# Scaled states on GpSimd, the output of the first units in two PSUM banks, and a new order of steps up to unit 6

## The chip, the core and the metric

The kernel runs on one core of a Trainium2 chip. TensorE (PE) multiplies, VectorE (DVE), ScalarE (ACT) and GpSimd (POOL) work elementwise, and the queue of SyncE (SP) issues nearly all DMA transfers. The metric is the device time of one execution in microseconds (us); less is better.

## The reference

A state-space attention (Mamba-2 style) of 4 batch rows, 8 heads, 768 tokens, head size 32 and state size 16, followed by a feed-forward layer with tanh-gelu on 3072 tokens:

```python
log_a = np.log(np.clip(a, 1e-06, 1.0))
for c in range(nc):                          # chunks of the sequence
    cum = np.cumsum(la, axis=-1)
    L = np.exp(cum[:, :, :, None] - cum[:, :, None, :]) * causal
    M = np.einsum('bhin,bhjn->bhij', Cc, Bc) * L
    y_intra = np.einsum('bhij,bhjd->bhid', M, xc)
    y_inter = np.einsum('bhin,bhnd->bhid', Cc, state) * np.exp(cum)[..., None]
    y[:, :, sl] = y_intra + y_inter
    state = decay_full * state + sum_over_j(B_j x_j * decay_from_j)
x = y.transpose(0, 2, 1, 3).reshape(3072, 256)
h = x @ w_in                                 # 256 -> 2048
g = 0.5 * h * (1.0 + np.tanh(c * (h + 0.044715 * h * h * h)))
out = g @ w_out                              # 2048 -> 256
```

Inputs and output are 32-bit floats; the products run in bf16 with 32-bit accumulation.

## The kernel before

The sequence is cut into 24 **chunks** of 128 tokens, 6 in each batch row, and 12 **units** of two chunks. Unit `u` holds chunks `2u` and `2u+1`; units 0 to 2 are batch 0, 3 to 5 batch 1, and so on. The decays are folded into B and C beforehand: a scan along the tokens gives the products of `a`, which scale B (with their value) and C (with their reciprocal).

The program is one list of steps, the string `ORDERED`. Each step issues its instructions on its engine when its turn comes, so the list sets the order of every engine and of SP's queue. A step's name is its function and its arguments; `:A`, `:D`, `:P`, `:S` after it name the engine (ACT, DVE, POOL, SP), and `@a`, `@b`, `@o`, `@y` the PSUM bank that it takes. Without a name, steps that ask for a passing bank get `bank_b` and `bank_a` in turn (`take`). Waits follow from what each instruction reads and overwrites.

The steps of unit `u`, with the lines of the profile:

- `G.u` (L637, L644, PE): products of B and C for 8 heads into the banks `ga` and `gb`. It needs `ce`, the masked C, and `bh`, B.
- `M.u.0`, `M.u.1` (L654, DVE): the causal mask on `ga` and on `gb`, to `m`.
- `castx.u` (L350, L352): x to bf16; `x` of units 0 and 1 is made on PE instead (`XX`, `XD`, `xn`).
- `D.u` (L679, PE): what the two chunks add to the state, from `bn` (B with tokens on the partitions) and x.
- `S.u.k` (L750, L752, DVE): the state after chunk `2u+k`. `SP.c` (L759, DVE): the state after chunk `c`, scaled by the decay and spread through the block mask `bmask` to 256 columns, so that one matmul on all 128 rows takes the part of one head. It needs `pendq` (chunks 0 to 2) or `pend`.
- `Y.u` (L701, L710, PE) for units 0 to 3: `m` times x, plus the state times `ce`, both into `bank_y`; `yev` (L348, ACT) copies it to `xm`. From unit 4 on `Yi` (L721) and `YI` (L734) do this for two units at once, in two banks.
- `s1.u.i` (L790 for units 0 to 3, L795 after): four matmuls of 256 columns (two of 512 later) with `w_in`; `gelu.u.i` (L801, L804, ACT) moves the result to `gT`; `s2.u.k.q` (L816) is a quarter of the product with `w_out` for chunk `k`: four matmuls of 256 columns; `oev.c` and `store.c` bring chunk `c` out.

Weights are loaded (`load_wi`, `load_wo`) and cast to bf16 (`wi`, `wo`). `s1.u.6` and `s1.u.7` need the last quarter of `w_in`.

The B and C of chunks 4 and 5 have steps of their own: the scan `R` (L365), its transpositions `tp2` and `tp6` (L375), `recip1`, the products `mul1.0` and `mul1.1` (L470), `T1.0`, `T1.1` (L478) and `N1` (L498) on PE, and the copies `ce1`, `bh1`, `bn1`; `pe`, `pp` and `pend` make the chunk-end decays of chunks 3 on. For batch 1 the steps are `mul`, `T`, `E`, `F`, `N`. For batches 2 and 3 they go through memory: `mul.b.1` and `mul.b.0` (L510) scale C and B, `load_wr.b.i` (L524) writes each to a scratch tensor, `load_tr.b.1` and `load_tr.b.0` (L531) read them back transposed as `ch` and `bh`, `load_bn.b` (L536) reads `bn`, and `F.b` (L549, DVE) makes `ce` from `ch`. `G.6` needs `ce` and `bh` of batch 2, `D.6` its `bn`; `D.9` is the first to need `bn` of batch 3.

`hold` (L630, GpSimd) copies one column of a scaled state, so that what follows on GpSimd waits for it.

Of the kernel before, what the change touches and what calls it, by code (L numbers as in the profile page):

```python
# [22 lines left out]
xn.2 s1.0.0 G.1 S.1.0 s1.0.1 xn.3 gelu.0.0 gelu.0.1 s1.0.2 gelu.0.2 M.1.1 wi.2.0 M.1.0 s1.0.3 gelu.0.3
s1.0.4 s1.0.5 recip1 S.1.1 gelu.0.4 gelu.0.5 SP.1 load_wi.3 wi.3.1 wi.3.0 load_bc1.1 s1.0.6 load_bc1.0
mul1.0:P SP.2 pe mul1.1:P T1.0 bh1:D tp6 Y.1 gelu.0.6 pp load_wo.0 pend:D yev.1.0.2 T1.1 N1 wo.0.0 s1.0.7
load_x.2 ce1.1:D castx.2.None ce1.0:D recip.1 s1.1.0 bn1 SP.3 gelu.0.7 wo.0.1 G.2 D.2 gelu.1.0 S.2.0
s1.1.1 gelu.1.1 s2.0.0.0 s1.1.2 gelu.1.2 s1.1.3 load_bc.1.1 SP.4 load_bc.1.0 M.2.1 M.2.0 gelu.1.3
load_wo.1 s2.0.1.0 mul.1.0 s1.1.4 hold.4 mul.1.1:P recip.2 load_x.3 gelu.1.4 wo.1.0 s1.1.5 wo.1.1 Y.2
gelu.1.5 castx.3.None s1.1.6 yev.2.0.2 T.1.0 s1.1.7 gelu.1.6 load_wo.2 E.1.0 T.1.1 s1.2.0 N.1 gelu.1.7
gelu.2.0 E.1.1 bn.1:D s1.2.1 F.1 s2.0.0.1 wo.2.0 wo.2.1:D s1.2.2 gelu.2.1 s2.0.1.1 D.3 G.3 S.3.0 gelu.2.2  # L30
s1.2.3 gelu.2.3 S.3.1 M.3.0 M.3.1 load_wo.3 load_x.4 wo.3.0:A s2.0.0.2 s2.0.1.2 wo.3.1 SP.6 s1.2.4 s1.2.5
castx.4.None s2.0.0.3 s2.0.1.3 gelu.2.4 gelu.2.5 oev.0:D s1.2.6 load_bc.2.1 load_bc.2.0 load_x.5 load_x.6
oev.1 SP.7 G.4 gelu.2.6 D.4 Y.3 yev.3.0.2:A s1.2.7 s2.1.0.0@o mul.2.1:P S.4.0 s2.1.1.0@y load_wr.2.1
s2.1.0.1 load_x.7 mul.2.0:P load_wr.2.0 load_tr.2.1 recip.3 load_bn.2 S.4.1 SP.9 M.4.1 load_tr.2.0
s2.1.0.2 gelu.2.7 s1.3.0 gelu.3.0 s1.3.1 s2.1.1.1 load_bc.3.1 gelu.3.1 s2.1.0.3 M.4.0 s1.3.2
castx.6.None:D load_bc.3.0 gelu.3.2 s1.3.3 gelu.3.3 s2.1.1.2 s2.1.1.3 s1.3.4 mul.3.1:P castx.5.None:D G.5
M.5.1 store.0 oev.2:A oev.3:A D.5 S.5.0 gelu.3.4 SP.10 s2.2.1.0@o load_x.8 store.1 s2.2.0.0@y s2.2.0.1
s2.2.0.2 SP.8 s1.3.5 gelu.3.5 s2.2.0.3 s1.3.6 castx.7.None:D M.5.0 gelu.3.6 s2.2.1.1 s2.2.1.2 store.3
s1.3.7 F.2 oev.4:A gelu.3.7 load_wr.3.1 load_x.9 Yi.4@ya Yi.5 YI.4 YI.5 G.6 D.6@b D.7 yew.4.1 s2.2.1.3
oev.5:D yew.4.0 s1.4.0@a S.6.0 S.6.1 S.7.0 s2.3.0.0@y gelu.4.0 S.7.1 M.6.0 SP.13 M.6.1 store.2 s1.4.1@o  # L40
mul.3.0:D load_wr.3.0 castx.8.None:D gelu.4.1 load_tr.3.1 s2.3.0.1 s1.4.2@a SP.12 s1.4.3@b s1.4.4@o
gelu.4.3 gelu.4.4 load_bn.3 gelu.4.2 load_tr.3.0 s2.3.0.2 s2.3.0.3 oev.6:A load_x.10 s1.4.5@b s1.4.6@o
# [24 lines left out]
oev.22:D store.22 oev.23:A store.23
# [15 lines left out]
def kernel(  # L83
# [113 lines left out]
    held = const.tile([128, 1], BF16, name="held")  # L197
# [430 lines left out]

    def f_hold(c):
        nc.gpsimd.tensor_copy(out=held, in_=state[("sp", c)][:, 0:1])  # L630
# [39 lines left out]
    def f_D(u):  # L670
# [3 lines left out]
        for k in range(2):  # L674
# [3 lines left out]
            for g in range(4):  # L678
# [404 lines left out]
```

## Time and profile before

| | us |
|---|---|
| three timed runs | 116.06, 116.80, 118.12 |
| median of them | 116.8 |
| span of the profiled execution, first to last instruction | 116.7 |
| PE busy in it | 107.8 |
| ACT busy | 69.8 |
| DVE busy | 66.2 |
| GpSimd busy | 24.8 |

No time of the profiled execution is given apart from its span; the span is 0.1 below the median of the timed runs. In a row of the profile `L816` is a line of the kernel, `out<-in` are its tiles, `x4` is the number of instructions merged into the row, and the brackets at a row's end hold the idle time before it and what ended that. PE's matmuls overlap, so what a step costs on PE is the distance from its start to the next one's, not the duration in its row. SPq is the queue of SP: its rows are the issuing of transfers, not the transfers.

### The profile page before, as it was taken

How to read it: one execution, taken by the hardware profiler on the slowest of the kernel's cores; microseconds unless marked ns; L12 is line 12 of the kernel's file. 1: busy time of each engine (PE TensorE's matmuls, PEld its weight loads, DVE VectorE, ACT ScalarE, POOL GpSimd, SP SyncE). 2: the span in 40 equal slices, each digit the busy share in tenths (PEclk: the TensorE clock that was granted, in tenths of full speed). 3: DMA queues.
4: the chain of work that ended last, by engine and by line, in shares of the span. 5: the costliest groups of instructions: out<-in, count | busy, mean ns of one | idle time of the engine just before them, and what ended most of it. 6: DMA issues, size and time to landing. Idle time of an engine off the chain costs nothing.

```text
span 116.7 us, 3120 instructions
## 1 busy us (share of the span) xinstructions
PE 107.8 (92%) x1276; PEld 77.6 (66%) x1284; DVE 66.2 (57%) x136; ACT 69.8 (60%) x135; POOL 24.8 (21%) x53
## 2 busy tenths in 40 slices
PE   6989758799999999999999999999999999999990
PEld 2345547588788969665766775777657676777870
DVE  3799995699899279399806901928614521011010
ACT  4179675587575655469774688834775565763500
POOL 7644737455526400050010200000000000000000
PEclk9999999999999999999999999999999999999999
DMA  0999949996997787895978802220000013301032
GB/s 26 254 313 314 305 81 239 286 230 178 296 249 117 144 168 152 201 248 170 217 145 142 169 3 93 96 90 6 0 0 0 0 51 123 101 0 45 6 135 90
DMA packets 43102, 15.99 MB, mean 137 GB/s; under 512 B 36688, under 2 KB 41552, under 8 KB 43088
## 3 DMA queue, kind: packets, MB, share of 16 engines
q1 hardware_dynamic: 42992, 15.76, 54.9%
q8 instruction: 10, 0.16, 0.7%
q10 hardware_dynamic: 96, 0.03, 0.1%
q14 instruction: 4, 0.03, 0.1%
HBM read 11.07 MB, written 3.93 MB: 129 GB/s over the span
## 4 chain that ended last, share of the span: by engine, by line
PE 52%; SPq 27%; DMA 14%; issue 2%; ACT 2%; DVE 0%; DVEq 0%
PE bank_y L816 13%; PE bank_o L816 12%; SPq L175 10%; PE bank_b L795 8%; SPq L194 7%; PE bank_a L795 6%; DMA wf<-in_moe_w_in_dram 5%; SPq L168 5%; DMA x_t<-in_x_dram 4%; PE bank_o L795 3%; DMA scr<-bc 2%; DMA bn<-scr 2%; PE bank_y L795 2%; PE bank_b L816 2%; PE bank_a L816 1%
## 5 line engine op out<-in xcount | busy, mean ns | idle before, releaser
L816 PEld LDWEIGHTS <-gT 128*128 128x128 bf16 x384 | 37.1, 98 | 10.4 <-issue 0.6
L816 PE MATMUL bank_o<-w_out_sb,gT 128*128 128x256 bf16 x192 | 26.1, 273 | 0.0
L816 PE MATMUL bank_y<-w_out_sb,gT 128*128 128x256 bf16 x160 | 21.2, 273 | 0.1
L795 PEld LDWEIGHTS <-w_in_sb 128*128 128x128 bf16 x128 | 14.2, 114 | 7.5 <-issue 0.4
L804 ACT ACTIVATE gT<-bank_b 128x512 bf16<-128x512 f32 x25 | 14.9, 597 | 6.5 <-PE bank_b L795 6.1
L654 DVE TENSOR_TENSOR m<-ga,tri 128x1024 bf16<-128x1024 f32 x12 | 14.6, 1218 | 5.2 <-PE gb L637 5.2
L804 ACT ACTIVATE gT<-bank_a 128x512 bf16<-128x512 f32 x21 | 12.6, 599 | 6.8 <-PE bank_a L795 2.5
L790 PEld LDWEIGHTS <-w_in_sb 128*128 128x128 bf16 x128 | 13.5, 114 | 4.1 <-POOL w_in_sb L350 1.6
L801 ACT ACTIVATE gT<-bank_b 128x512 bf16<-128x512 f32 x17 | 10.1, 597 | 8.7 <-PE bank_b L790 8.6
L795 PE MATMUL bank_b<-xm,w_in_sb 128*128 128x512 bf16 x48 | 14.5, 380 | 0.2
L654 DVE TENSOR_TENSOR m<-gb,tri 128x1024 bf16<-128x1024 f32 x11 | 13.4, 1216 | 0.0
L790 PE MATMUL bank_b<-xm,w_in_sb 128*128 128x256 bf16 x68 | 10.3, 274 | 1.7 <-POOL w_in_sb L350 1.3
L795 PE MATMUL bank_a<-xm,w_in_sb 128*128 128x512 bf16 x36 | 11.2, 380 | 0.1
L352 DVE COPY o_sb<-bank_y 128x256 f32<-128x256 f32 x5 | 2.1, 425 | 15.7 <-PE bank_y L816 13.7
L801 ACT ACTIVATE gT<-bank_a 128x512 bf16<-128x512 f32 x15 | 8.9, 595 | 3.4 <-PE bank_a L790 3.3
L790 PE MATMUL bank_a<-xm,w_in_sb 128*128 128x256 bf16 x60 | 9.0, 273 | 0.9 <-ACT gT L801 0.4
L759 DVE SCALAR_TENSOR_TENSOR sp_new<-s_new,pend,bmask 128x256 bf16<-128x256 f32 x17 | 8.2, 497 | 0.3 <-DVE s_new L752 0.2
L352 DVE CAST xm<-bank_a 128x512 bf16<-128x512 f32 x4 | 2.8, 692 | 9.7 <-PE bank_a L734 9.7
L773 PE MATMUL bank_y<-wz 128*128 128x512 bf16 (+2 forms) x20 | 7.1, 499 | 1.1 <-DVE warm L225 1.1
L510 POOL TENSOR_TENSOR bc<-bc_t,pt 128x768 bf16<-128x768 f32 x3 | 4.7, 1563 | 14.6 <-PE bank_o L795 11.6
L804 ACT ACTIVATE gT<-bank_o 128x512 bf16<-128x512 f32 x10 | 6.0, 597 | 2.4 <-PE bank_o L795 2.3
L348 ACT ACTIVATE xm<-bank_y 128x512 bf16<-128x512 f32 x8 | 4.8, 596 | 3.8 <-PE bank_a L734 3.5
(149 smaller groups left out, 130.9 us busy)
## 6 DMA issues: line engine op xcount, KB each, us to landing
out_dram<-o_sb SPq DMA_DIRECT2D x24, 128.0 KB, 1.8
x_t<-in_x_dram SPq DMA_DIRECT2D x20, 128.0 KB, 4.3
wf<-in_moe_w_in_dram SPq DMA_DIRECT2D x4, 512.0 KB, 6.4
wf<-in_moe_w_out_dram SPq DMA_DIRECT2D x4, 512.0 KB, 6.5
bc_t<-in_C_dram SPq DMA_DIRECT2D x3, 384.0 KB, 6.9
bc_t<-in_B_dram SPq DMA_DIRECT2D x3, 384.0 KB, 6.3
scr<-bc SPq DMA_DIRECT2D x4, 192.0 KB, 3.0
x_t<-in_x_dram SPq DMA_DIRECT2D x1, 512.0 KB, 5.0
```

The lines of the kernel that those rows point to most:

```text
L168: nc.sync.dma_start(out=d["bc"][:, i], in_=(B, C)[i][b].rearrange("h (p r) n -> p h (r n)", r=R6))
L175: (nc.scalar if eng == "ACT" else nc.sync).dma_start(out=XF[u][:, k], in_=x[b, :, (c + k) * Q:(c + k + 1) * Q, :].rearrange("h p d -> p h d"))
L194: nc.sync.dma_start(out=WF[("o", q)], in_=wo[q])
L352: nc.vector.tensor_copy(out=o, in_=i)
L654: nc.vector.tensor_tensor(out=m_of(u)[:, 2 * i:2 * i + 2].rearrange("p g k e t -> p (g k e) t"), in0=gx[i].rearrange("p g (k t) -> p (g k) ...
L759: nc.vector.scalar_tensor_tensor(out=sp_new.rearrange("p (g d) -> p g d", g=4), in0=(XN[0][:, H * D:H * D + 64] if gc == 0 else state[("s" ...
L773: nc.tensor.matmul(out=t[:, 0:m * 128], lhsT=wz, rhs=w3.to_broadcast([128, m, 128]), start=True, stop=True, skip_group_check=True)
L790: nc.tensor.matmul(out=hp[:, j * T:(j + 1) * T], lhsT=w_in_k[:, w, q, k], rhs=xm[:, w, u * T:(u + 1) * T], start=(w == 0), stop=(w == 1))
L795: nc.tensor.matmul(out=hp, lhsT=w_in_k[:, w, q, k], rhs=xm[:, w, u * T:u * T + PT], start=(w == 0), stop=(w == 1))
L801: nc.scalar.activation(gts[u][:, 2 * i:2 * i + 2], hp.rearrange("p (j t) -> p j t", j=2), AF.Gelu_apprx_tanh)
L804: nc.scalar.activation(gts[("p", u)][:, i], hp, AF.Gelu_apprx_tanh)
L816: nc.tensor.matmul(out=ops[gc], lhsT=gts[u][:, fi, k * Q:(k + 1) * Q], rhs=w_out_sb[:, fi, :], start=(fi == 0 and (u > 0 or k == 0)), stop ...
```

## The change

Four things change; everything from `Yi.4` on stands in the order of before.

- `SP` of chunks 1 to 4 no longer spreads the state through the mask. It scales the 64 columns alone, on GpSimd. The matmuls that use it take 32 rows of it each, at the row group of their head.
- `Y` of units 0 to 2 goes into two banks, one for heads 0 to 3 and one for heads 4 to 7, and `yev` is two copies, one on ACT and one on DVE.
- The scan `R` stands behind the masks of unit 1 (`M.1.1`, `M.1.0`) on DVE.
- The list of steps up to `Yi.4` is in a new order. The `s1` steps of units 0 to 3 take four banks by name, and those of unit 1 begin before those of unit 0 have ended. `hold` is gone.

```diff
-xn.0:D load_wi.2 SP.0 ~13 Y.0 wi.0.1:A wi.0.0:A S.0.0 clip R S.0.1 yev.0.0.2 ...
+xn.0:D load_wi.2 SP.0 S.0.0 ~13 Y.0@ya wi.0.1:A wi.0.0:A clip S.0.1 yev.0.0.1:A yev.0.1.2:D G.1 SP.1:P
...
 def f_N1():
-        T0[2] = gx[0][:, 1].bitcast(BF16)[:, 0:n * 128]
+        T0[2] = take("hp").bitcast(BF16)[:, 0:n * 128]
...
-    def f_hold(c):
-        nc.gpsimd.tensor_copy(out=held, in_=state[("sp", c)][:, 0:1])
...
+    def f_Y2(u):
+        YT[u] = [t[:, 0:T].rearrange("p (k t) -> p k t", t=Q)
+                 for t in ((take("y"), take("hp")) if u == 0 else (yb, gx[1][:, 1]))]
...
+        sps = [state.pop(("sp", 2 * u + k - 1)) for k in range(2)]
+        for k, j, w in [(k, j, w) for k in range(2) for j in range(4) for w in range(2)]:
+            h = 4 * w + j
+            gs = slice(32 * (h // 2), 32 * (h // 2) + 32)
+            nc.tensor.matmul(out=YT[u][w][32 * j:32 * j + 32, k],
+                             lhsT=sps[k][gs, 32 * (h % 2):32 * (h % 2) + 32], rhs=ce_of(2 * u + k)[gs, h % 2],
+                             start=first(j, w), stop=False, tile_position=(32 * (h // 2), 32 * j),
+                             skip_group_check=True)
+        for k in range(2):
+            intra(k)
...
     def f_yev(u, w0, w1, eng):
+        if u < 3:
+            copy(eng, xm[:, w0, u * T:(u + 1) * T], YT[u][w0].rearrange("p k t -> p (k t)"))
+            return
...
-    def f_SP(gc):
+    def f_SP(gc, eng):
+        if 0 < gc < 5:
+            sn = st.tile([128, 64], BF16, name="sn")
+            if eng == "ACT":
+                nc.scalar.activation(sn, state[("s", gc)], AF.Copy, scale=pend_of(gc + 1))
+            else:
+                (nc.gpsimd if eng == "POOL" else nc.vector).tensor_scalar(
+                    out=sn, in0=state[("s", gc)], scalar1=pend_of(gc + 1), scalar2=None, op0=ALU.mult)
+            state[("sp", gc)] = sn
+            return
```

SP's queue where batch 2 goes through memory, before. `x_t_773`, `x_t_776` and `x_t_847` are `load_x.5`, `.6` and `.7`; `scr21` and `scr20` are the scratch tensors of C and B of batch 2, `bc_t_884` is the input of batch 3:

```order
L175 DMA x_t_773<-in_x_dram 128x8x32 x2
L175 DMA x_t_776<-in_x_dram 128x8x32 x2
L524 DMA scr21_841<-bc16_833 128x768
L175 DMA x_t_847<-in_x_dram 128x8x32 x2
L524 DMA scr20_851<-bc16_833 128x768
L531 DMA_TRANSPOSE ch_853<-scr21_841 128x768
L536 DMA bn_856<-scr20_851 128x6x128
L531 DMA_TRANSPOSE bh_864<-scr20_851 128x768
L168 DMA bc_t_884<-in_C_dram 128x8x96
L168 DMA bc_t_884<-in_B_dram 128x8x96
```

The same place now, where `x_t_784`, `x_t_913` and `x_t_918` are `load_x.5`, `.6` and `.7`, `scr21_871` and `scr20_916` the scratch tensors, and `bc_t_951` the input of batch 3:

```order
L177 DMA x_t_784<-in_x_dram 128x8x32 x2
L525 DMA scr21_871<-bc16_869 128x768
L177 DMA x_t_913<-in_x_dram 128x8x32 x2
L525 DMA scr20_916<-bc16_869 128x768
L177 DMA x_t_918<-in_x_dram 128x8x32 x2
L532 DMA_TRANSPOSE ch_921<-scr21_871 128x768
L170 DMA bc_t_951<-in_C_dram 128x8x96
L532 DMA_TRANSPOSE bh_953<-scr20_916 128x768
L537 DMA bn_955<-scr20_916 128x6x128
L170 DMA bc_t_951<-in_B_dram 128x8x96
```

Both writes to scratch stand one load of x earlier, C of batch 3 stands ahead of `bh`, and `bn` behind `bh`. Ahead of this place the queue is the same in both kernels.

GpSimd's queue from the first cast of `w_in` to the cast of `x.2`, before (`bc0s1` is the result of `mul1`, `x16` that of `castx`):

```order
L350 CAST w_in_sb_138<-wf_235 128x512 x2
L350 CAST w_in_sb_138<-wf_305 128x512 x2
L350 CAST w_in_sb_138<-wf_446 128x512 x2
L470 TENSOR_TENSOR bc0s1_131<-bcf1_95,rt01_123 128x256
L470 TENSOR_TENSOR bc0s1_131<-bcf1_95,pt01_125 128x256
L350 CAST w_out_sb_139<-wf_500 128x512
L350 CAST x16_518<-x_t_514 128x512
```

And now (`sn` are the scaled states `SP.1`, `SP.2` and `SP.3`):

```order
L806 TENSOR_SCALAR sn_353<-s_new_341,pendq_127 128x64
L351 CAST w_in_sb_137<-wf_234 128x512 x2
L806 TENSOR_SCALAR sn_415<-s_new_413,pendq_127 128x64
L351 CAST w_in_sb_137<-wf_304 128x512 x2
L351 CAST w_in_sb_137<-wf_427 128x512 x2
L471 TENSOR_TENSOR bc0s1_130<-bcf1_95,rt01_122 128x256
L351 CAST w_out_sb_138<-wf_431 128x512 x2
L806 TENSOR_SCALAR sn_547<-s_new_418,pend_128 128x64
L351 CAST x16_559<-x_t_509 128x512
```

Three scaled states and the second cast of `w_out` have come in ahead of the cast of `x.2`, and `mul1.1` has gone to DVE.

DVE's queue behind the clip of `a`, before (`r_t` is the scan `R`, `m_422` the masks `M.1.1` and `M.1.0`):

```order
L362 TENSOR_SCALAR ac_104<-a_t_93 128x256
L365 SCALAR_TENSOR_TENSOR r_t_106<-ac_104,ends_102 128x256
L752 SCALAR_TENSOR_TENSOR s_new_343<-s_new_339,pendq_128,bank_b_144 128x64
L375 STREAM_TRANSPOSE rt01_123<-r_t_106 32x64 x4
L752 SCALAR_TENSOR_TENSOR s_new_408<-s_new_343,pendq_128,bank_a_143 128x64
L654 TENSOR_TENSOR m_422<-gb_142,tri_112 128x1024
L654 TENSOR_TENSOR m_422<-ga_141,tri_112 128x1024
```

And now (`xm` is the half of `yev` that DVE does):

```order
L363 TENSOR_SCALAR ac_103<-a_t_93 128x256
L795 SCALAR_TENSOR_TENSOR s_new_341<-s_new_308,pendq_127,bank_b_143 128x64
L353 CAST xm_139<-bank_a_142 128x256
L652 TENSOR_TENSOR m_405<-gb_141,tri_111 128x1024
L795 SCALAR_TENSOR_TENSOR s_new_413<-s_new_341,pendq_127,bank_b_143 128x64
L652 TENSOR_TENSOR m_405<-ga_140,tri_111 128x1024
L795 SCALAR_TENSOR_TENSOR s_new_418<-s_new_413,pendq_127,bank_o_144 128x64
L366 SCALAR_TENSOR_TENSOR r_t_105<-ac_103,ends_101 128x256
L353 CAST xm_139<-gb_141 128x256
L376 STREAM_TRANSPOSE rt01_122<-r_t_105 32x64 x4
```

The scan and its transpositions have moved behind both masks, and the copies of `yev` have come in.

More of the change, by code (lines that the diff above doesn't have):

```diff
@@ L23 @@
[L23 to L42, printed above, removed]
@@ new lines @@
+s1.1.1@y gelu.1.1 mul1.1:D mul1.0:P pe s1.1.2@a gelu.1.2 load_x.2 T1.1 ce1.1:D ce1.0:A s1.1.3@b gelu.1.3
+T1.0 bh1:D pp@o pend:D s1.0.6@y gelu.0.6 wo.0.0 wo.0.1 N1@o bn1:D G.2 M.2.1 SP.3:P s1.0.7@a gelu.0.7
+s1.1.4@b gelu.1.4 castx.2.None D.2@o S.2.0 SP.4:P M.2.0 s1.1.5@y gelu.1.5 tp6 load_bc.1.1 load_bc.1.0
+recip.1 s2.0.0.0@o s1.1.6@a gelu.1.6 load_wo.1 Y.2 s2.0.1.0 yev.2.0.1:A yev.2.1.2:D s1.1.7@b gelu.1.7
+recip.2 load_x.3 s1.2.0@a gelu.2.0 s1.2.1@y gelu.2.1 mul.1.1:P mul.1.0 load_wo.2 s1.2.2@b gelu.2.2 T.1.1
@@ L1009 @@
             yis[u - 1].takes("o", yev[u - 1][1])
-    hold = add("P", f_hold, 4, deps=[SPn[4]])
-    steps["mul.1.1"].deps.append(hold)
     s1, gel, s2, oev = {}, {}, {}, {}
```

107 lines of the change are left out of this document (74 added, 33 removed).

## The prediction

> **What bounds the kernel now.** I began with the page: the length of the execution and the share of the engine that fills it.
>
> ```profile
> span 116.7 us, 3120 instructions
> ...
> PE 107.8 (92%) x1276; PEld 77.6 (66%) x1284; DVE 66.2 (57%) x136; ACT 69.8 (60%) x135; POOL 24.8 (21%) x53
> ```
>
> PE is busy 92% of the span, but that is an average, so next come two stages of the table by windows (window, its length, busy time of PE, PEld, DVE, ACT, POOL, granted clock, DMA share, GB/s).
>
> ```profile
> 100.00:110.00 10.00, 9.95 (x75) 7.50 (x75) 0.85 (x2) 5.32 (x10) 0.00 (x0) 1.00 0.07 23
> ...
> 113.60:116.70 3.10, 0.00 (x0) 0.00 (x0) 0.00 (x0) 0.38 (x1) 0.00 (x0) 1.00 0.24 85
> ```
>
> Late in the kernel PE has no gap, and the tail after its last matmul is 3.1 us of output. The order after `Yi.4` is the same in both kernels. So the end moves by what PE has gained when it comes to the head of unit 4, and by nothing else. What PE waits for says what can be gained there.
>
> ```profile
> PE bank_b L790 <- POOL w_in_sb L350: 1.3, 1, 1.3
> ...
> PE bank_b L679 <- POOL x L350: 0.7, 1, 0.7
> ...
> PE bank_a L679 <- DVE x L352: 0.3, 1, 0.3
> PE bank_b L679 <- DMA bn<-scr: 0.2, 1, 0.2
> ```
>
> Each row is one wait. The timeline of PE puts them in their places.
>
> ```profile
> 17.87 0.63 PE L790 MATMUL bank_b<-xm,w_in_sb 128*128 128x256 bf16 x4 [1.31 <-POOL w_in_sb L350]
> ...
> 21.91 0.21 PE L679 MATMUL bank_b<-x,bn 128*32 128x64 bf16 x4 [0.73 <-POOL x L350]
> ...
> 22.96 0.60 PE L790 MATMUL bank_b<-xm,w_in_sb 128*128 128x256 bf16 x4
> 23.40 0.60 PE L790 MATMUL bank_a<-xm,w_in_sb 128*128 128x256 bf16 x4
> ...
> 47.97 0.29 PE L637 MATMUL ga<-ce,bh 32*64 32x256 bf16 x2
> ...
> 48.32 0.30 PE L679 MATMUL bank_b<-x,bn 128*32 128x64 bf16 x16
> ...
> 61.69 0.24 PE L679 MATMUL bank_b<-x,bn 128*32 128x64 bf16 x8 [0.20 <-DMA bn<-scr]
> ```
>
> 17.87 is `s1.0.6`, which needs the last quarter of `w_in`; 21.91 is `D.2`, which needs the cast of `x.2`; 47.97 is `G.6`, 48.32 is `D.6` with `D.7`, 61.69 is `D.9`. One `s1` step of four matmuls takes 23.40 - 22.96 = 0.44 us, and so does a quarter of `s2`, which is also four matmuls of 256 columns.
>
> **The change, part by part.**
>
> *PE up to `D.2`.* The SP queue is the same in both kernels up to `load_x.5`, so the loads land when they did. GpSimd's timeline shows the casts that wait for them.
>
> ```profile
> 16.64 1.18 POOL L350 CAST w_in_sb<-wf 128x512 bf16<-128x512 f32 x2 [1.82 <-DMA wf<-in_moe_w_in_dram]
> 17.78 0.62 POOL L470 TENSOR_TENSOR bc0s<-bcf,rt 128x256 bf16<-128x256 f32 x1
> ...
> 21.13 0.73 POOL L350 CAST x<-x_t 128x512 bf16<-128x512 f32 x1 [1.16 <-DMA x_t<-in_x_dram]
> 23.24 0.19 POOL L630 COPY held<-sp_new 128x1 bf16<-128x1 bf16 x1 [0.82 <-DVE sp_new L759]
> ```
>
> `x.2` is still cast at 21.13 to 21.86, and `D.2` still starts at 21.9. What is new is the work that PE has behind it by then. Counted in the two orders, `D.2` had 9 `s1` steps ahead of it (8 of unit 0, 1 of unit 1) and now has 13 (8 and 5). Four steps of 0.44 make 1.75 us that no longer lie in the waits at 17.87 and 21.91 and in those for gelu, where only banks a and b took turns. Does PE finish them by 21.9? Its last need before is `mul1.0`: on GpSimd it follows the cast that ends at 17.82, and at 0.62 it ends at 18.44. From there `T1.0`, the copy of `bh` on VectorE, `pp`, `pend` and `N1` take until about 19.4, an estimate; then come `G.2` at 0.33, `s1.0.7` and `s1.1.4`, to about 20.6. That leaves 1.3 us of slack, so the later decay scan and the mask of unit 1, now ahead of it on VectorE, cost nothing. If they came out 1.3 us later still, the gain would begin to shrink one for one.
>
> *GpSimd's scaled states.* Four such operations of 128x64 are new there and no row shows one. They lie between the copy of 128x1 at 0.19 and the product of 128x256 at 0.62; I take 0.25, as 64 columns are nearer the former. `SP.1` and `SP.2` stand ahead of `w_in` casts that wait for landings anyway, and `SP.3` waits for `pend` at 19.4 and ends, with both `wo.0` casts ahead of it, before `x.2` lands. I cost them at nothing: the landings hide them, at 0.62 as well. `hold` goes, and nothing waited for it but GpSimd's queue. On VectorE four masked copies of about 0.4 to 0.5 us go, in a stretch where PE waits for loads.
>
> *Y in two banks.* Its evacuation is split over ScalarE and VectorE, so the first `s1` step of a unit starts a little sooner; the matmuls on 32 rows instead of 128 can run side by side. No row shows that form with 128 columns. I bound the saving by 0 and 0.2 us for each of the units 1 and 2, and take 0, since PE waits for a landing soon after both.
>
> *From `D.2` to `G.6`.* The wait of 0.3 us goes: `D.5` waited for a cast that stood on VectorE behind that of `x.6`; now GpSimd casts `x.5` right after `mul.2.0`, at about 39.2, two microseconds before PE needs it. One quarter of `s2` (`s2.2.1.2`) moves from ahead of `Yi.4` to behind `D.7`: PE comes 0.44 sooner and owes it later. So PE alone comes to `G.6` at 47.97 - 1.75 - 0.3 - 0.44 = 45.5.
>
> *What `G.6` and `D.6` wait for.* `G.6` needs `bh` and `D.6` needs `bn` of batch 2, which go through memory: scaled on GpSimd, written, read back. First GpSimd, then the SP queue (start, time that the issue took).
>
> ```profile
> 36.03 1.70 POOL L510 TENSOR_TENSOR bc<-bc_t,pt 128x768 bf16<-128x768 f32 x1 [2.29 <-DMA bc_t<-in_C_dram]
> 37.69 1.49 POOL L510 TENSOR_TENSOR bc<-bc_t,rt 128x768 bf16<-128x768 f32 x1
> ```
>
> ```profile
> 27.36 1.06 SPq L175 DMA_DIRECT2D x_t<-in_x_dram  x2
> 28.46 2.54 SPq L168 DMA_DIRECT2D bc_t<-in_C_dram  x1
> ...
> 38.48 2.61 SPq L175 DMA_DIRECT2D x_t<-in_x_dram  x2
> 41.18 0.57 SPq L524 DMA_DIRECT2D scr<-bc  x1
> 42.12 1.24 SPq L531 DMA_TRANSPOSE ch<-scr  x1
> 44.44 0.39 SPq L536 DMA_DIRECT2D bn<-scr  x1
> 44.88 1.23 SPq L531 DMA_TRANSPOSE bh<-scr  x1
> 46.21 0.53 SPq L168 DMA_DIRECT2D bc_t<-in_C_dram  x1
> ```
>
> And from issue to landing, by the DMA view of the windows around three of these (line, size, us):
>
> ```profile
> scr<-bc SPq DMA_DIRECT2D x1, 192.0 KB, 3.2
> bn<-scr SPq DMA_DIRECT2D x1, 192.0 KB, 2.7
> bh<-scr SPq DMA_TRANSPOSE x1, 3.0
> ```
>
> Now: `bn` is issued at 44.44, when the write issued at 41.18 has landed (44.4), and lands at 47.1; `bh` lands at 44.88 + 3.0 = 47.9. `G.6` starts at 47.97. PE and this chain arrive together: there is no slack that the change could use.
>
> In the new order `mul.2.0` still ends at 39.18, since its loads and GpSimd's queue have not moved. The second write no longer stands behind `load_x.7`, so it can be issued at 39.2 instead of 41.18. But `load_x.7`, the reading of `ch`, and `load_bc.3.1` come between it and `bh`, and `bn` comes after `bh`. With every issue at its unblocked duration: 39.2 + 0.57 + 1.06 + 1.24 + 0.53 = 42.6 for `bh`, which lands at 45.6; 42.6 + 1.23 = 43.8 for `bn`, which lands at 46.5. That is the floor of `D.6`. With `load_x.7` blocked as at 38.48 (1.55 more) and `load_bc.3.1` blocked as at 28.46 (2.0 more) `bn` lands at 50.1, the ceiling. What decides is how full the DMA engines are:
>
> ```profile
> 30.00:32.00 2.00, 2.00 (x31) 1.45 (x29) 1.68 (x5) 1.10 (x3) 1.46 (x2) 1.00 1.25 258
> ...
> 36.00:40.00 4.00, 4.00 (x39) 3.74 (x38) 2.64 (x3) 1.68 (x3) 3.15 (x2) 1.00 0.79 150
> 40.00:44.00 4.00, 3.71 (x42) 2.95 (x41) 2.35 (x5) 2.29 (x5) 0.00 (x0) 1.00 0.69 141
> ```
>
> Their share is 1.25 at the end of the blocked issue at 28.46, and 0.79 and 0.69 in the stretch in question. That is nearer to the unblocked rows, so I take a quarter of the way up: `D.6` at 47.4.
>
> **The sum.** `D.6` goes from 48.32 to 47.4, 0.9 less; the owed quarter takes 0.44 back; the wait of 0.2 at 61.69 goes, because the chain of `load_bn.3` follows the SP queue, whose issue of `load_bc.3.0` ended at about 47.3 (46.21 + 0.53 + some 0.57) and now ends at about 45.7 (43.8, 0.9 of backlog, 0.39 for `bn`, 0.57). 0.9 - 0.44 + 0.2 = 0.7 us less. The profiled span of 116.7 becomes 116.0; the median of the three timed runs, 116.8, lies 0.1 above that span, so I forecast **116.1 us**. Most of what PE gains in its first 45 us is given back as about 1.5 us of waiting at `G.6` and `D.6` (47.4 - 45.5 - 0.35 for `G.6`).
>
> **Rivals.**
>
> *All of PE's gain counts.* If the chain of batch 2 lands before 45.5 and 45.9, the end moves by 1.75 + 0.3 + 0.2, and by up to 0.2 for the 32-row matmuls: 2.4 us, 114.4. Against it: the floor for `bn` is 46.5 with every issue unblocked. For it: the loads of `x.6` leave the queue ahead of the first write, and the transfers may land faster than the 2.7 and 3.0 us above.
>
> *Pinned by the next chain.* `D.9` stood at 61.69 because `bn` of batch 3 landed then. If that landing doesn't move, because VectorE's `mul.3.0` or the stores ahead of `load_wr.3.0` hold it, nothing is gained whatever happens before: 116.8.
>
> *Slower, by the new place of `load_bc.3.1` and `load_x.7`.* From `bn` landing after 48.1 on (48.32 - 0.44 + 0.2) the kernel loses. At the ceiling, 50.1, it loses 2.0: 118.8. Then PE is idle for over 3.6 us ahead of `G.6`, and something that the start of this trace shows may add to it:
>
> ```profile
> 1.07 4.85 PE L773 MATMUL bank_y<-wz 128*128 128x512 bf16 x12 [1.07 <-DVE warm L225]
> ...
> 49.87 0.59 PE L795 MATMUL bank_o<-xm,w_in_sb 128*128 128x512 bf16 x2
> 50.30 0.60 PE L816 MATMUL bank_y<-w_out_sb,gT 128*128 128x256 bf16 x4
> ```
>
> The first twelve matmuls of 512 columns, after an idle start, take 0.40 us each; at 49.87 two of them take 0.43 together. Twelve at the slow rate lose 2.2 us, so this case reaches 121.0. The Trainium skill ("TensorE: Matmul & The Clock Gate", Part 1: The HAM clock gate) says that after an idle window of about 3.4 us the array falls to half its clock until it has been busy for about as long. By that rule the wait of 1.5 us that I forecast costs nothing more; the trace agrees so far as it goes, since the matmuls after the wait of 1.31 at 17.87 run at 0.44 for four.
>
> **How the numbers follow.** My forecast has a chance of 0.60 and its own range is 115.2 (`bn` at the floor) to 117.0; all of PE's gain 0.13, 114.4; pinned 0.10, 116.8; slower by the queue 0.17, 117.0 to 121.0. A measurement of this kernel tells 2% from no change, that is 2.3 us. Faster by over 2% is under 114.5, most of the first rival: 0.10. Slower by over 2% is over 119.1, the upper part of the last: 0.07. The rest is 0.83. The range from 114.4 to 118.5 leaves out about 0.15, nearly all at its upper end.
>
> **What would show it.** `D.2` at 21.9 as before, with 13 `s1` steps ahead of it; `Yi.4` at about 44.5 instead of 46.98; a wait of PE for `bh` or `bn` of about 1.5 us in all just behind it; `D.6` at 47.4; no wait at `D.9`; from there every step some 0.7 us earlier. I am wrong if PE comes to `G.6` later than 47, which would mean waits for gelu, VectorE or GpSimd that I have not seen; if `G.6` does not wait at all; or if `D.6` comes after 48.1.

## The result, and the profile after

| | us |
|---|---|
| four runs of the changed kernel | 119.68, 119.94, 120.38, 121.50 |
| median of them | 120.16 |
| kernel before, same chip | 116.78 |
| ratio to the kernel before, 95% interval | 1.029 (1.024 to 1.034) |
| span of the profiled execution | 119.7 |

The ratios and intervals, here and below, leave out runs more than 1.5% above the fastest of the same kernel, while the medians are of all runs, so the two can differ by a few tenths of a per cent. The changed kernel is slower by 3.4 us; the forecast was 116.1 us, with 114.4 to 118.5 as its range. The profiled execution of the changed kernel is the longest of the four (121.5 us), so it is checked further down against a later profile of the same kernel. Its page, busy time of each engine:

```profile
span 119.7 us, 3121 instructions
...
PE 109.5 (91%) x1276; PEld 78.0 (65%) x1284; DVE 66.6 (56%) x132; ACT 67.9 (57%) x134; POOL 29.2 (24%) x60
```

PE is busy 1.7 us longer than before with the same number of matmul records (1276), so matmuls have become slower somewhere. Next what PE waits for (total, number, longest), the rows that answer to those of before:

```profile
PE ga L635 <- DMA bh<-scr: 1.7, 1, 1.7
PE bank_o L677 <- POOL x L351: 1.4, 1, 1.4
...
PE bank_b L677 <- DMA bn<-scr: 0.6, 1, 0.6
PE ga L642 <- DVE bn L353: 0.5, 1, 0.5
```

The timeline of PE puts them in place: `D.2`, the end of `YI.5`, `G.6`, `D.6`, and the matmuls behind it.

```profile
22.26 0.21 PE L677 MATMUL bank_o<-x,bn 128*32 128x64 bf16 x4 [1.39 <-POOL x L351]
...
46.64 0.22 PE L774 MATMUL bank_a<-ch,sp_new 32*64 32x128 bf16 x2
48.60 0.30 PE L635 MATMUL ga<-ce,bh 32*64 32x256 bf16 x2 [1.75 <-DMA bh<-scr]
...
49.62 0.30 PE L677 MATMUL bank_b<-x,bn 128*32 128x64 bf16 x16 [0.59 <-DMA bn<-scr]
...
51.83 1.06 PE L868 MATMUL bank_y<-w_out_sb,gT 128*128 128x256 bf16 x4 [0.22 <-issue]
```

PE would have come to `G.6` at 48.60 - 1.75 = 46.85 and waited there for `bh`, then 0.59 us at `D.6` for `bn`. `D.6` starts at 49.62; 47.4 was forecast. And four matmuls at 51.83 take 1.06 us where before they took 0.60. The windows name the reason (the third column from the right is the granted clock):

```profile
46.00:48.00 2.00, 0.86 (x48) 0.59 (x40) 1.38 (x4) 1.18 (x2) 0.12 (x1) 1.00 1.23 209
48.00:50.00 2.00, 0.81 (x34) 0.47 (x35) 0.00 (x0) 0.00 (x0) 1.38 (x1) 1.00 1.30 243
50.00:52.00 2.00, 1.78 (x10) 1.22 (x10) 0.74 (x3) 0.00 (x0) 0.00 (x0) 0.62 1.43 192
52.00:54.00 2.00, 2.00 (x9) 1.12 (x8) 1.93 (x5) 0.82 (x2) 0.00 (x0) 0.53 0.60 169
```

Behind the two waits the clock is halved. Cut into quarters of a microsecond, it is 0.50 from 50.5 to 53.9. Last, SP's queue, from the second write to scratch on, and the landings of that write, of `bh` and of `bn`:

```profile
38.20 0.52 SPq L525 DMA_DIRECT2D scr<-bc  x1
38.77 1.67 SPq L177 DMA_DIRECT2D x_t<-in_x_dram  x2
40.53 3.02 SPq L532 DMA_TRANSPOSE ch<-scr  x1
43.66 0.52 SPq L170 DMA_DIRECT2D bc_t<-in_C_dram  x1
44.23 1.27 SPq L532 DMA_TRANSPOSE bh<-scr  x1
45.55 0.57 SPq L537 DMA_DIRECT2D bn<-scr  x1
```

```profile
scr<-bc SPq DMA_DIRECT2D x1, 192.0 KB, 4.9
bh<-scr SPq DMA_TRANSPOSE x1, 4.3
bn<-scr SPq DMA_DIRECT2D x1, 192.0 KB, 4.0
```

The write leaves earlier than before (38.20 instead of 41.18) and that is all the new order gains. It lands 4.9 us later instead of 3.2, `bh` 4.3 instead of 3.0, `bn` 4.0 instead of 2.7, so `bn` is there at 49.55.

### The profile page after: what moved, and what is told of

The parts are those of the page before. It is cut to its first block, busy times and chain, and to the rows that moved or that the text cites. A ratio compares the mean times of both kernels' runs of the same rounds, so it can differ in the third digit from the quotient of the medians.

```text
span 119.7 us, 3121 instructions
## 1 busy us (share of the span) xinstructions
PE 109.5 (91%) x1276; PEld 78.0 (65%) x1284; DVE 66.6 (56%) x132; ACT 67.9 (57%) x134; POOL 29.2 (24%) x60
## 4 chain that ended last, share of the span: by engine, by line
PE 62%; DMA 14%; DVE 11%; SPq 8%; issue 1%; POOL 1%; ACT 0%; DVEq 0%; POOLq 0%
PE bank_o L868 15%; PE bank_y L868 12%; PE bank_b L847 9%; PE bank_a L847 7%; DMA wf<-in_moe_w_in_dram 5%; DMA x_t<-in_x_dram 5%; PE bank_o L847 4%; DVE m L652 4%; DMA bn<-scr 3%; SPq L196 3%; PE bank_y L847 3%; PE bank_a L868 3%; PE bank_b L868 3%; DVE bc L511 1%; PE ga L635 1%
## 5 line engine op out<-in xcount | busy, mean ns | idle before, releaser
L868 PE MATMUL bank_o<-w_out_sb,gT 128*128 128x256 bf16 x176 | 24.2, 275 | 0.0
L856 ACT ACTIVATE gT<-bank_b 128x512 bf16<-128x512 f32 x25 | 15.0, 598 | 6.7 <-PE bank_b L847 6.2
L856 ACT ACTIVATE gT<-bank_a 128x512 bf16<-128x512 f32 x21 | 12.6, 599 | 10.3 <-PE bank_o L868 5.7
L868 PE MATMUL bank_y<-w_out_sb,gT 128*128 128x256 bf16 x128 | 17.6, 279 | 0.3 <-issue 0.2
L351 POOL CAST x<-x_t 128x512 bf16<-128x512 f32 x8 | 5.1, 642 | 21.3 <-DMA x_t<-in_x_dram 8.7
L853 ACT ACTIVATE gT<-bank_a 128x512 bf16<-128x512 f32 x11 | 6.6, 601 | 3.6 <-PE bank_a L842 3.6
L353 DVE COPY o_sb<-bank_o 128x256 f32<-128x256 f32 x5 | 2.1, 421 | 10.5 <-PE bank_o L868 7.3
L353 DVE CAST xm<-bank_a 128x512 bf16<-128x512 f32 (+1 forms) x5 | 3.2, 636 | 8.2 <-PE bank_a L774 8.2
L349 ACT ACTIVATE xm<-bank_y 128x512 bf16<-128x512 f32 (+1 forms) x8 | 4.1, 514 | 6.3 <-PE bank_y L750 3.2
L811 DVE SCALAR_TENSOR_TENSOR sp_new<-s_new,pend,bmask 128x256 bf16<-128x256 f32 x15 | 7.4, 518 | 0.0
L842 PE MATMUL bank_a<-xm,w_in_sb 128*128 128x256 bf16 x44 | 6.7, 274 | 0.4 <-ACT gT L853 0.4
L853 ACT ACTIVATE gT<-bank_b 128x512 bf16<-128x512 f32 x9 | 5.4, 601 | 2.4 <-PE bank_b L842 2.4
```

The source lines that it names most:

```text
L349: nc.scalar.activation(o, i, AF.Copy)
L351: nc.gpsimd.tensor_copy(out=o, in_=i)
L353: nc.vector.tensor_copy(out=o, in_=i)
L811: nc.vector.scalar_tensor_tensor(out=sp_new.rearrange("p (g d) -> p g d", g=4), in0=(XN[0][:, H * D:H * D + 64] if gc == 0 else state[("s" ...
L842: nc.tensor.matmul(out=hp[:, j * T:(j + 1) * T], lhsT=w_in_k[:, w, q, k], rhs=xm[:, w, u * T:(u + 1) * T], start=(w == 0), stop=(w == 1))
L853: nc.scalar.activation(gts[u][:, 2 * i:2 * i + 2], hp.rearrange("p (j t) -> p j t", j=2), AF.Gelu_apprx_tanh)
```

## The experiments

Theory Q: the loss is made in SP's queue around batch 2, and shows as the waits of 2.34 us and the lower clock behind them. Theory F: it is made earlier, by the new front. The names of transfers are those of the list of steps; "the order of before" means that order in SP's queue alone.

### The queue of before

```diff
-load_bc.2.1 load_bc.2.0 load_x.5 s2.1.0.2 ...
+load_bc.2.1 load_bc.2.0 load_x.5 load_x.6 s2.1.0.2 ...
-... mul.2.0:P load_x.6 load_wr.2.0 load_x.7 load_tr.2.1 G.5 ...
+... load_x.7 mul.2.0:P load_wr.2.0 load_tr.2.1 load_bn.2 load_tr.2.0 G.5 ...
-... load_bc.3.1 load_tr.2.0 load_bn.2
+... load_bc.3.1
```

> The changed kernel, with the transfers of batch 2 on SP's queue in the order that they had before: the load of x.6 ahead of wr.2.1, x.7 between wr.2.1 and wr.2.0, then tr.2.1, bn.2, tr.2.0, and C and B of batch 3 behind them. Theory Q (the loss is made in SP's queue around wr.2.0, and all of it is G.6's and D.6's waits of 1.75 and 0.59 us and the lower clock behind them): wr.2.0 lands in about 3 us instead of 4.9, bn and bh land before 46, G.6 waits less than 0.2 us, D.6 starts at 46.9 to 47.5, the granted clock stays 1.00 from 50 to 54, and the time is 115.8 to 117.0 us. Theory F (the loss is made earlier, by GpSimd's states and DVE slowing each other, and PE's waits only show it): the waits go, but the time stays at 118.5 us or more.

Measured: 116.47 us beside 116.17 for the kernel before, ratio 1.000 (0.996 to 1.004). In the profiled execution PE does not wait for `bh` or `bn` at all, and the clock stays at 1.00. The landings (the time from issue until the data is there) of `bn` and `bh`, and `D.6`:

```profile
bn<-scr SPq DMA_DIRECT2D x1, 192.0 KB, 2.7
bh<-scr SPq DMA_TRANSPOSE x1, 3.2
```

```profile
46.24 0.30 PE L677 MATMUL bank_b<-x,bn 128*32 128x64 bf16 x16
```

So the whole loss is in the queue and in what follows from it, and F falls. But the gain of 0.7 us that I had forecast isn't there either: with the queue of before, the change is worth nothing that this interval can show.

### The kernel before, with the queue of after

```diff
-load_x.5 load_x.6
+load_x.5
-... load_x.7 mul.2.0:P load_wr.2.0 load_tr.2.1 recip.3 load_bn.2 ... load_tr.2.0
+... mul.2.0:P load_x.6 load_wr.2.0 load_x.7 load_tr.2.1 recip.3 ... load_bc.3.1 load_tr.2.0 load_bn.2
-s2.1.0.2 gelu.2.7 ... s2.1.1.1 load_bc.3.1 gelu.3.1 ...
+s2.1.0.2 gelu.2.7 ... s2.1.1.1 gelu.3.1 ...
```

> The kernel before, with nothing changed but the places of four loads on SP's queue, as the change has them: x.6 between wr.2.1 and wr.2.0, x.7 behind wr.2.0, C of batch 3 ahead of tr.2.0, and bn.2 behind it. Theory Q: D.6 moves from 48.3 to 50 to 51.5, since wr.2.0 is issued at 41.2 here and bn three transfers later, the granted clock drops below 0.7 for some us behind it, and the time is 119 to 122 us. Theory F: the order of the queue is not what costs, D.6 moves by less than 0.7 and the time stays within 116.0 to 117.5 us.

Measured: 117.24 us, ratio 1.010 (1.006 to 1.013), and no dip of the clock. That is less than Q expected, and inside the range that I had given to F. The waits of PE say why:

```profile
PE bank_a L679 <- DVE x L352: 1.3, 1, 1.3
...
PE bank_b L679 <- DMA bn<-scr: 0.6, 1, 0.6
```

Here VectorE casts `x.6` ahead of `x.5`, so the later load of `x.6` holds `D.5` for 1.3 us, and PE comes that much later to `G.6`; only 0.6 us is left to wait there. The landings of `bh` and `bn` are 4.2 and 4.0 us, as in the changed kernel. The order of the queue costs the kernel before 1.1 us. It costs the changed kernel more, where both waits lie close together and the clock falls around them.

### C of batch 3 behind `bn`

```diff
-... load_bc.3.1 load_tr.2.0 load_bn.2
+... load_tr.2.0 load_bn.2 load_bc.3.1
```

> The changed kernel, with the load of C of batch 3 moved from ahead of tr.2.0 to behind bn.2, and nothing else. If the queue is slow by what x.6 and x.7 put into it, bh is issued 0.5 to 0.6 us earlier and no more, the waits shrink from 2.3 to 1.7 us, and the time is 118.5 to 119.7, with the clock's dip. If the place of C of batch 3 is what costs (as the rival of the prediction had it), the waits shrink by 1.5 us or more, no dip is left, and the time is 116.5 to 117.5.

Measured: 116.85 us, ratio 1.006 (1.001 to 1.010): most of the loss gone by moving one transfer of 384 KB. The loads of `x.6` and `x.7` still stand where the change put them, and the second write still takes 4.3 us to land. What is left is this wait, and these landings:

```profile
46.24 0.30 PE L677 MATMUL bank_b<-x,bn 128*32 128x64 bf16 x16 [0.91 <-DMA bn<-scr]
```

```profile
bh<-scr SPq DMA_TRANSPOSE x1, 2.7
bn<-scr SPq DMA_DIRECT2D x1, 192.0 KB, 3.0
```

My reading by `x.6` and `x.7` (1.7 us of wait left) is refuted; the place of C of batch 3 is what costs. In all six profiles with C ahead, those of the runs below among them, `bh` takes 4.2 to 4.3 us to land and `bn` 3.9 to 4.0. With C behind, five profiles have 2.7 to 3.2 and 2.7 to 3.0; in three (the states on VectorE, and the last two of the search for a gain, below) `bh` takes 3.6 to 4.3 and `bn` 3.2 to 3.3, so something else can lengthen them too, which I have not traced. Here, where nothing but C has moved, it is C.

### Zeros in the two waits

```diff
-            fill(yb, int(w[1:]))
+            fill(bank["b"] if w[1] == "b" else yb, int(w.lstrip("~b")))
-Yi.4@ya Yi.5 YI.4 YI.5 G.6 D.6@b D.7 ...
+Yi.4@ya Yi.5 YI.4 YI.5 ~b30 G.6 ~b8 D.6@b D.7 ...
```

> The changed kernel, with matmuls of zeros on TensorE (30 of 128 columns ahead of G.6, 8 between G.6 and D.6, about 0.054 us each, 2.0 us in all) that read the constant weights wz, are overwritten by D.6 and lie in the two waits. Theory H (the idle time of TensorE lowers the clock behind it, a term of its own): D.6 starts at 49.5 to 49.9 as before, the granted clock stays 1.00 from 50 to 54, and the time falls by about 1.7 us, to 118.0 to 118.9. Rival (the clock falls for another reason, such as a disturbance, or the load of all engines): the dip of 3.4 us stays, and the time is 119.7 to 120.6.

Measured: 118.37 us, ratio 1.021 (1.014 to 1.029). The dip is gone from the profiled execution, and the median is 1.8 us below that of the four runs above; but the changed kernel had not run beside it. What did run beside it, on the same chip, is the version with C behind, at 1.006 and with a profile without a dip too; so the place of C costs 1.6% there, without any part of the clock. From the issue of the second write to the landing of `bn` it is 44.22 + 4.0 - 37.68 = 10.5 us here and 43.21 + 3.0 - 37.23 = 9.0 there: about 0.5 for the issue of C, and 1.0 for the longer landing.

Then the changed kernel again, unaltered:

> The changed kernel itself, unaltered, beside the kernels that follow. Theory Q, now with its price (C of batch 3 ahead of tr.2.0 lengthens the landing of bh from 2.7 to 3.2 us to 4.2 to 4.4 and that of bn from 2.7 to 3.0 us to 4.0): the two landings are 4.1 to 4.5 and 3.8 to 4.2 us again, G.6 and D.6 wait 2 us or more together, the granted clock dips behind them to 0.5 to 0.6 for 3 to 4 us, and the ratio to the kernel before is 1.022 to 1.035. Rival (the first profile of the changed kernel was an outlier): waits under 1 us, no dip, and a ratio under 1.015.

Measured: 120.23 us, ratio 1.024 (1.016 to 1.031); landings of 4.2 and 3.9 us, waits of 1.83 and 0.51 us, the clock at 0.50 for 3.4 us. Then both on one chip, with more rounds:

> The changed kernel itself, on the chip of the three kernels that follow, so that they can be set against it. Ratio to the kernel before 1.022 to 1.033; bh landing 4.2 to 4.4 us after its issue, bn 3.9 to 4.1, G.6 and D.6 waiting 2.0 to 2.5 us together, and the granted clock at 0.50 for 3.4 us (3.41 and 3.42 in its two traces) from some point 2 to 4 us behind the first idle microsecond.

> The same with the matmuls of zeros in G.6's and D.6's waits (the third experiment), beside the changed kernel on one chip. Theory H (the half clock is a cost of its own, brought on by the idle time): no clock below 1.00 behind D.6, D.6 to the end 68.2 to 68.6 us against 69.5 to 70.1 in the changed kernel, and 1.0 to 1.8 us less than the changed kernel: ratio to the kernel before 1.010 to 1.019. Rival (the clock matters little, since what follows waits for something else): less than 0.6 us below the changed kernel, ratio 1.020 or more.

Measured: 119.30 us, ratio 1.027 (1.022 to 1.032) for the changed kernel, and 118.53, ratio 1.018 (1.015 to 1.022) with the zeros. The intervals only meet at 1.022. `D.2` and `D.6` of the changed kernel, and `D.6` with the zeros, each with its span:

```profile
span 117.8 us, 3121 instructions
```

```profile
20.66 0.21 PE L677 MATMUL bank_o<-x,bn 128*32 128x64 bf16 x4
...
48.12 0.41 PE L677 MATMUL bank_b<-x,bn 128*32 128x64 bf16 x16 [0.59 <-DMA bn<-scr]
48.46 1.89 PE L868 MATMUL bank_o<-w_out_sb,gT 128*128 128x256 bf16 x8
```

```profile
span 116.7 us, 3140 instructions
```

```profile
48.30 0.30 PE L677 MATMUL bank_b<-x,bn 128*32 128x64 bf16 x16
48.53 1.05 PE L868 MATMUL bank_o<-w_out_sb,gT 128*128 128x256 bf16 x8
```

From `D.6` to the end it is 117.8 - 48.12 = 69.7 us without the zeros and 116.7 - 48.30 = 68.4 with them. So the half clock costs 1.3 us in this pair of executions: eight matmuls right behind `D.6` take 1.89 us instead of 1.05. In the first profile, where all of the 3.4 us at half clock lie behind `D.6`, the same stretch is 119.7 - 49.62 = 70.1 us, 1.7 more than with the zeros. By the medians it is 0.8; there the zeros end late, since `bn` lands at 47.8 in that profile and `D.6` stands behind them until 48.3.

The mean granted clock of every run is on record as well; a dip of 3.4 us brings it to 0.986. It lies below 0.99 in 12 of the 14 runs of the changed kernel, in 1 of 10 with the zeros, and in 6 of 135 of all other kernels, the kernel before included. So the idle time goes with the dip, but does not bring it each time. The two runs of the changed kernel without it took 118.84 and 119.20 us, the four beside them with it 119.13 to 120.47. By these few runs the dip is worth 0.4 us, less than by the profiles, and most of the loss is there without it. No trace of these two was kept, so why they escaped it is open, and so is the price of the dip in a typical run, between 0.4 and 1.7 us.

### The kernel before, a second profile

> The kernel before itself, unaltered, for a second profile. Theory S (the stalls of 1.31 and 0.73 us up to D.2 in its first profile, which the forecast counted as gained by the change, were late loads of that one execution): none of the two is there, D.2 starts at 19.7 to 20.5 instead of 21.91, D.6 at 45.6 to 46.6 instead of 48.32, span 113.9 to 115.0. Rival (the stalls belong to the kernel): D.2 stands at 21.4 to 22.2 and D.6 at 47.8 to 48.6.

Measured: 116.03 us in one execution. The page, `D.2` and `D.6`:

```profile
span 114.3 us, 3120 instructions
```

```profile
20.31 0.21 PE L679 MATMUL bank_b<-x,bn 128*32 128x64 bf16 x4 [0.17 <-POOL x L350]
...
46.24 0.30 PE L679 MATMUL bank_b<-x,bn 128*32 128x64 bf16 x16
```

The stall of 1.31 us is not there, and of that of 0.73 only 0.17 is left. They were late loads of the one execution from which I had forecast. Its span, 116.7, was 2.4 longer than this one, and longer than that of each of the 64 runs of the kernel before beside these experiments (113.6 to 116.4, median 114.5). It only looked like the median of the runs because about 1.7 us outside the span belong to a run (116.03 - 114.3); that the two agreed was luck. Against 46.24, the changed kernel comes to `D.6` at 48.12 - 1.75 - 0.59 = 45.78, and 0.44 of that is the quarter of `s2` that it owes. In this pair of executions the new front (the order up to `Yi.4`) is worth 0.02 us.

### Looking for a gain of the front

All three start from the queue of before. First the owed quarters and their eviction ahead of `G.6`:

```diff
-YI.4 YI.5 G.6 D.6@b D.7 yew.4.1 s2.2.1.2 s2.2.1.3 oev.5:D yew.4.0
+YI.4 YI.5 s2.2.1.2 s2.2.1.3 oev.5:D G.6 D.6@b D.7 yew.4.1 yew.4.0
```

> The changed kernel with the transfers of batch 2 in the order of before (as in the first experiment), and the two owed quarters s2.2.1.2 and s2.2.1.3 (0.88 us of TensorE) with the eviction oev.5 moved ahead of G.6, so that they lie in what is left of the wait for bh and bn. If the new front (states on GpSimd, Y in two banks, the new order) is worth the 0.7 us that the forecast gave it, nothing waits at G.6 and D.6 and the time is 0.992 to 0.996 of the kernel before. If the front is worth nothing (its gain was the removal of stalls that the kernel before does not usually have), the ratio is 0.998 to 1.004.

Measured: 116.56 us, ratio 1.003 (0.999 to 1.007). The eviction now holds VectorE's part of `xm`, and PE waits for that instead:

```profile
47.26 0.41 PE L847 MATMUL bank_a<-xm,w_in_sb 128*128 128x512 bf16 x1 [0.53 <-DVE xm L353]
```

With that eviction back behind the two of `xm`:

```diff
-YI.4 YI.5 s2.2.1.2 s2.2.1.3 oev.5:D G.6 D.6@b D.7 yew.4.1 yew.4.0
+YI.4 YI.5 s2.2.1.2 s2.2.1.3 G.6 D.6@b D.7 yew.4.1 yew.4.0 oev.5:D
```

> The changed kernel with the transfers of batch 2 in the order of before and the quarters s2.2.1.2 and s2.2.1.3 ahead of G.6, with oev.5 left behind the evictions yew.4.1 and yew.4.0. In the experiment with oev.5 ahead of them the first s1 step of unit 4 waited 0.53 us for VectorE's part of xm. If that wait hid a gain of the front, it goes, and the time falls by 0.3 to 0.5 us, to 0.996 to 1.000 of the kernel before; if the front has no gain to show, 1.000 to 1.004.

Measured: 115.99 us beside 116.28, ratio 0.997 (0.994 to 1.000); the wait for `xm` is gone. And with a copy of batch 1 moved from VectorE to ScalarE in addition:

```diff
-E.1.1 T.1.0 E.1.0 F.1
+E.1.1 T.1.0 E.1.0:A F.1
```

> As the kernel before this one, and the copy of bh of batch 1 (E.1.0, 0.94 us of VectorE) moved to ScalarE, since VectorE's row of mul.1.0 (1.85 us beside GpSimd's own product, 0.95 before), two copies and F.1 is what G.3 waits 0.47 us for in the new order. If that is the part of the front that eats its gain, G.3's wait goes and the time falls by a further 0.3 to 0.5 us, to 0.992 to 0.997 of the kernel before. If ScalarE's gelu steps are delayed by as much, or the gain is lost behind it at another wait, the ratio is 0.998 to 1.003.

Measured: 115.98 us, ratio 0.998 (0.996 to 1.001). The further gain that I had hoped for from `G.3` is not there: `G.3` waits 0.3 us in this profile, and 0.2 in that of the version without the move, so there was little to take. The first of these two is the best version found, 0.3% below the kernel before, but its interval just includes no change.

One thing that the front pays for is shown by VectorE's rows for batch 1, first in the second profile of the kernel before, then in the changed kernel of the pair:

```profile
23.76 0.96 DVE L510 TENSOR_TENSOR bc<-bc_t,rt 128x768 bf16<-128x768 f32 x1
...
27.54 0.74 DVE L549 TENSOR_SCALAR ce<-ch,par 128x768 bf16<-128x768 bf16 x2
```

```profile
23.91 1.85 DVE L511 TENSOR_TENSOR bc<-bc_t,rt 128x768 bf16<-128x768 f32 x1
25.68 0.94 DVE L353 COPY ch<-gb 128x768 bf16<-128x768 bf16 x1
...
27.41 1.38 DVE L550 TENSOR_SCALAR ce<-ch,par 128x768 bf16<-128x768 bf16 x2
```

In the new order GpSimd works all through this stretch; its product and its casts:

```profile
23.45 1.50 POOL L511 TENSOR_TENSOR bc<-bc_t,pt 128x768 bf16<-128x768 f32 x1 [1.61 <-DVE pt L416]
24.89 1.90 POOL L351 CAST w_out_sb<-wf 128x512 bf16<-128x512 f32 x2
...
27.29 2.53 POOL L351 CAST w_out_sb<-wf 128x512 bf16<-128x512 f32 x4
```

VectorE's product and mask take twice as long beside it, while the copy from PSUM takes no longer. The Trainium skill ("GPSIMD Engine Reference", 1. Specifications) says that the two engines share their way into SBUF and get into each other's way when VectorE reads two SBUF inputs or runs in a mode with two ports; the product has two such inputs, and the trace agrees. Behind that stands the wait of 0.5 us at `G.3` in the three profiles of the changed kernel. As the last two versions had only 0.2 and 0.3 of it, it is not shown to be what eats the gain.

### The states on VectorE

```diff
-SP.1:P ... SP.2:P ... SP.3:P ... SP.4:P
+SP.1:D ... SP.2:D ... SP.3:D ... SP.4:D
```

> The changed kernel with the transfers of batch 2 in the order of before, and the scaled states SP.1 to SP.4 (four operations of 128x64) on VectorE instead of GpSimd. If GpSimd's four operations of 0.44 us delay its casts and so TensorE (D.2's wait on the cast of x), D.2 starts 0.3 us or more earlier than with GpSimd and the time falls to 115.5 to 116.1 us. If VectorE is the tighter engine up to G.3 (56% to 99% busy there), the four operations delay M.1, M.2 and S, D.2 and G.3 come 0.2 us or more later, and the time is 116.6 to 117.5 us. If neither, it is within 0.3 us of the first experiment's 116.4.

Measured: 117.37 us, ratio 1.007 (1.003 to 1.011), against 116.47 with the states on GpSimd and the same queue. VectorE's masks come later, and PE waits at `Y.1`:

```profile
15.41 0.24 PE L698 MATMUL bank_y<-m,x 128*32 128x128 bf16 x4 [0.86 <-DVE m L652]
...
22.02 0.21 PE L677 MATMUL bank_o<-x,bn 128*32 128x64 bf16 x4
```

`D.2` starts at 22.02, later than in all other profiles of this front that did not wait there for the cast of `x.2` (20.46 to 21.41, the latter in the first experiment). The two ratios, 1.007 here and 1.000 there, have intervals that overlap a little, and the two ran on different chips; so GpSimd is the better engine for the four states by the waits, and by the time probably.

## Why the prediction was wrong

**PE up to `D.2`: right in what it counted, wrong in what that was worth.** `D.2` has 13 `s1` steps ahead of it and starts at 22.26, 0.35 later than before, as it waits for the cast of `x.2` again. But the 1.75 us were measured against stalls that the kernel before does not usually have. Without those, `D.2` moves from 20.31 to 20.66, so the four steps gain 1.4 there.

**GpSimd's scaled states: sized too low, without harm.** I took 0.25 us; the four took 0.44 each, within the bounds, and by the last experiment they are probably cheaper there than on VectorE.

**From `D.2` to `G.6`: failed.** Forecast 45.5, found 46.85. Of the 1.35 us, 0.35 is `D.2`; 0.5 is `G.3`, which waits behind VectorE's slowed product and mask; 0.2 is a wait at `T.1.0`. The rest is 0.3 here. Between the two later profiles it is 0.9: 1.4 gained at `D.2` and 0.2 at `D.5`, less the 0.02 that is left and the 0.7 of `G.3` and `T.1.0`. It is spread over gaps too small for the list of waits, and I have not settled it.

**What `G.6` and `D.6` wait for: the step that failed.** The mechanism was right, a chain through memory with no slack, and the second write was issued even earlier than forecast (38.2, 39.2 forecast). The size was off. I had put every landing at its duration of before and looked for trouble only in the issues, a quarter of the way from the floor to the ceiling, because the DMA share at that place was 0.79 and 0.69 in the old order. The new order puts 384 KB just ahead of `bh` and `bn`: from 46 to 50, while they are in flight, the share is 1.23 to 1.30. Issued at 45.55 instead of 44.7, landed after 4.0 instead of 2.7, `bn` came 2.1 us later than forecast. The issues were late at another place than the two that I had allowed for: `load_bc.3.1` took its unblocked 0.52, but the reading of `ch`, which I had put at 1.24, held the queue for 3.02. That alone did not make the loss: with the zeros and the same queue it was 1.81 in one profile and 3.07 in the other, at ratios of 1.021 and 1.018.

**The clock: the second term that failed.** I had let 1.5 us of waiting cost nothing more, and kept the cost of the clock to a wait of over 3.6. The clock fell after a first wait of 1.75 us, 0.4 us of matmuls and a second wait of 0.59 in the first profile, and in the two later ones already before the second wait. The Trainium skill ("TensorE: Matmul & The Clock Gate", Part 1: The HAM clock gate) gives an idle window of about 3.4 us as the condition, and says that the window of 3.413 us runs free of the kernel. The length of the dip agrees, 3.4 us in all profiles of the changed kernel; the condition does not. In the last of them the clock falls at 47.4, after 1.75 us of idle time and 0.3 us of `G.6`:

```profile
47.00:47.25 0.25, 0.15 (x13) 0.15 (x16) 0.00 (x0) 0.00 (x0) 0.25 (x1) 1.00 1.35 236
47.25:47.50 0.25, 0.25 (x16) 0.01 (x2) 0.00 (x0) 0.00 (x0) 0.25 (x1) 0.87 1.29 227
47.50:47.75 0.25, 0.03 (x8) 0.00 (x0) 0.00 (x0) 0.00 (x0) 0.25 (x1) 0.50 1.28 232
```

What the three falls share is that PE was idle for more than half of the time ahead of them: of the 3.41 us before each it was busy 1.29, 1.58 and 1.66. But 1.68 of 3.41, ahead of the end of the wait of 1.31 in the first profile of the kernel before, brought no fall, so these profiles do not settle what the condition is.

**The sum.** In the profile that answers to the forecast `D.6` came 2.2 us late, and from there to the end it took 70.1 instead of 68.6: together the 3.7 between the forecast span of 116.0 and 119.7. Between the two later profiles, from 114.3 to 117.8, it is the two waits 2.34, the half clock 1.3, and 0.2 less from the front and the quarter that moved (0.46 gained ahead of `D.6`; 0.3 paid behind it, as the first experiment's 114.6 - 46.24 = 68.4 stands to 68.1 before). The wait at `D.9` is not there, as forecast, but the second profile of the kernel before does not have it either.

**The rivals.** What happened is the third, slower by the new place of `load_bc.3.1` and `load_x.7`, to which I gave 0.17 and 117.0 to 121.0. The loads are now told apart in part: the place of the first costs 2.1 to 2.7 us (1.006 instead of 1.024 to 1.029), the clock's part included. The rest, about 0.6, belongs to the places of `x.6` and `x.7` and to `bn` behind `bh` together (1.000 instead of 1.006, with intervals that overlap); these were not tried one by one.

## What to carry to other kernels

A load that nothing urgent waits for can still be the costliest instruction in the queue, if it stands ahead of a transfer that is waited for: price it by what it does to the landings behind it, not by its own issue. Before counting a stall as a gain, find it in a second execution; one that comes from a late load may be the execution's, not the kernel's. And a wait of PE of two microseconds can cost up to another 1.7 us behind it, so when a chain has no slack, keep work at hand that can stand in the gap.

## What the runs showed of the hardware

- With a load of 384 KB issued just ahead, a transposed read of 192 KB landed after 4.2 to 4.3 us and a plain read after 3.9 to 4.0, in six profiles; with that load alone moved behind them, after 2.7 and 3.0, in one. In three other profiles with the load behind, the transposed read took 3.6 to 4.3 as well.
- A granted clock of 0.50 for 3.4 us, each time as long, went with a wait of 1.75 to 1.83 us, 0.4 to 0.5 us of matmuls and a second wait of 0.51 to 0.59. In two profiles it began before the second wait, in the third behind it, and two of 14 runs of this kernel had none. A single wait of 1.31 us, 1.39 or 0.91 brought none in the profiles.
- A transposed read issued behind loads of x held the queue for 3.0 to 3.2 us in the three profiles of the changed kernel, for 1.8 and 3.1 with the zeros in the same queue, and for 1.2 before. What it waits for there was not tried.
- VectorE's product of 128x768 took 1.85 us beside GpSimd's work and 0.96 alone.
